# Chunked attention and a low-rank mixer on one core: W2's odd blocks moved, sums split by product, turns in place, attention's order placed anew

## The chip, the cores and the metric

The kernel runs on one core of a Trainium2 chip. The metric is the device time of one execution in microseconds (us); the median of 3 runs of the kernel before is 1055.16 us (1054.91 to 1055.36).

## What is computed

Attention within chunks of 64 positions, for 8 batches, 8 heads, 576 positions and a head size of 64; its output, 576 x 512 per batch, is x of a mixer. The mixer adds a product of rank 32 along the positions, then a two-layer ReLU network along the 512 channels with 2048 hidden ones:

```python
scores = scale * np.matmul(q_c, k_c.transpose(0, 1, 2, 4, 3))
scores = scores - np.max(scores, axis=-1, keepdims=True)
attn = np.exp(scores)
attn = attn / (np.sum(attn, axis=-1, keepdims=True) + 1e-09)
out = np.matmul(attn, v_c)
...
h = xt @ U @ V
u = x + h.transpose(0, 2, 1)
ch = np.maximum(u @ w_ch1, 0.0) @ w_ch2
return (u + ch).astype(np.float32)
```

q, k and v are float32; U, V and both weights come as float64 words and are turned to float32 in the kernel.

## The kernel before

**Tiles and groups.** Two batches make a pair (pr 0 to 3) of 1152 rows: nine tiles of 128 rows, three groups of three tiles. The hidden channels are 16 blocks f of 128. Every float32 product is made as three products in the matmul's float32r type: each operand is split into a high part (ScalarE, ACT, copies it) and the rest (VectorE, DVE, subtracts), and high x high, high x low and low x high are summed in a PSUM bank.

**Stages.** Pair 0's attention, the conversion of the weights and pair 0's first two groups come first, in an order that a planner inside the kernel makes (`order`, L144). From then on the program runs in ticks. `agenda` (L1042) is a dictionary from a tick to functions; `at` (L1046) enters one, and `tick` (L1180) runs those of the current tick after each step of TensorE (PE). So a tick is a place in the program's order, and with that a place in the queue of every engine; it is no time. Each engine, and each engine's queue of DMA issues, works in this order, and what waits holds all that is behind it. Ticks 128 to 256 run group (0, 2) and group (1, 0), 16 blocks each of `hidden` (L887, 12 matmuls) and `project_out` (L913, 9 matmuls), from weights that stay in SBUF.

**Joints.** The other eight groups are worked two at a time in four joints of 128 ticks each (`joint`, L1188; JOINT, L1074), from tick 256 to 768. There the first layer is a 2 x 2 block product with seven products in place of eight (1 to 7; the step A1 is product 1 of pair of blocks A). A joint has four chunks; a chunk has 14 such products of six matmuls (L1280) and 12 steps Ga, Gb of the second layer (L1257). Both operands of the seven products are sums of blocks. Those of W1 are made once: `combos` (L1080) has GpSimd (POOL) make the sums (L1098 to L1103), ACT and DVE split them (L1108, L1109), and SP (SyncE's queue) stores them to memory as `wc` (L1110); `plain_parts` (L1117) stores the blocks that need no sum. All eight use one pair of rooms, with 512 of each room's columns for the sums and 512 for their high parts. In the joints these operands are streamed back, 368 blocks in all through 11 windows (`window`, L1126; `issue`, L1134). Seven windows are two pieces of SBUF, the end of W1's area in an even and in an odd block, so a block takes two transfers (L1141); four are one piece (L1144).

The operands of u live in the first part of the same areas (`combo`, L1149). `u_combos` (L1153) makes them for one tile of the next joint: four sums on POOL (L1170 to L1173), then for each of the seven a copy (L1177) and a subtraction (L1178). Between two joints it is called three times, in the last chunk, after the steps Gb0, Ga2 and Ga3 (L1296).

**Attention of pairs 1 to 3** runs beside all this. `permute` (L681) rewrites q and k in memory by blocks of 32, issued from ACT. A tile (class Tile, L695) is loaded (L705), turned on DVE from qn to qT and kn to kT (L713), and at a visit (`visit`, L1312, at the ticks of VISITS, L1302) scored (L730); its softmax follows on DVE and ACT (L739). `turn_ex` (L759) turns ex into exb; `put_ex` (L765) stores it and `get_ex` (L772) reads it back as eT, both from SP; `load_v` (L715) is issued from POOL. At the next visit `values` (L779) takes eT, and `scaled` (L792) gives x. `spill` (L802) stores x; `fetch` (L841) reads it back for the mixer's sum `add` (L649), after which `turn` (L855), `put` (L862) and `get` (L869) bring u into shape, and `store` (L845) keeps it until `residual` (L1192) reads it as xr. The tiles of attention and of the mixer (qn, kn, qT, kT, ex, exb, vn, eT, xh, xl, xb, uf, us) come from one pool of nine slots, x from one of nine; a tile of a pool waits until the tile that last had its place is done with.

## Time and profile before

| what | value |
|---|---|
| median of 3 runs | 1055.16 us |
| the profiled execution's own time | 1051.83 us |
| its span | 1050.1 us |
| mean granted TensorE clock | 0.935 |
| PE, DVE, ACT, POOL busy, share of the span | 88%, 56%, 29%, 16% |
| DMA | 198.77 MB, mean 189 GB/s |

Times in the profile are microseconds from the start of the span. PE is TensorE's matmuls, PEld its weight loads, SPq (ACTq, POOLq) the DMA issues of that engine's queue. A granted clock of 1.00 is 2.4 GHz and 0.50 is 1.2 GHz; a value between them is a mean over a stretch. An engine's idle time is put down to what released it. The profiled execution is one execution; its durations are used for the sums, and its own time lies 3.33 us below the median.

### The profile page before, as it was taken

To read this page: it belongs to the slowest core of one execution; us is meant where nothing else is said; L and a number is where in the kernel's file an instruction comes from. 1 tells how busy PE (TensorE), PEld (TensorE's weight loads), DVE (VectorE), ACT (ScalarE), POOL (GpSimd) and SP (SyncE) were. 2 spreads that over 40 slices of the span, in tenths; PEclk is the share of its full clock that TensorE was granted. 3 is DMA by queue.
4 is the path that set the end of the run, shared out by engine and by line. 5 is a ranking of instruction groups with operands and counts; after the bars stand their busy time and mean duration, and the time that the engine had idled before them with its cause. 6 is when DMAs were issued, how large, how long until landed. Compare 5 with 4: busy or idle time off the path is not lost.

```text
span 1050.1 us, 17589 instructions
## 1 busy us (share of the span) xinstructions
PE 924.7 (88%) x6404; PEld 805.6 (77%) x6404; DVE 589.2 (56%) x1142; ACT 306.1 (29%) x600; POOL 167.6 (16%) x253
## 2 busy tenths in 40 slices
PE   6899999985869698978599778888978999999998
PEld 5689888764757587967498667777867988899987
DVE  5899965662546366645355474546664444753333
ACT  5666621221212013312022141222233221522211
POOL 4200001345441013201000140101050000300000
PEclk9999999987879889988799889988989999999999
DMA  9975857567779975969776896837669447674311
GB/s 185 219 248 157 223 107 152 150 190 173 184 232 285 267 216 157 288 166 246 173 209 168 224 275 168 225 95 206 183 208 278 153 132 210 210 240 139 111 62 61
DMA packets 362789, 198.77 MB, mean 189 GB/s; under 512 B 214384, under 2 KB 327568, under 8 KB 362704
## 3 DMA queue, kind: packets, MB, share of 16 engines
q1 hardware_dynamic: 247104, 174.78, 58.0%
q10 hardware_dynamic: 111360, 14.16, 8.8%
q0 software_dynamic: 4240, 8.71, 3.0%
q8 instruction: 51, 0.84, 0.3%
q14 instruction: 34, 0.28, 0.1%
HBM read 145.93 MB, written 65.80 MB: 202 GB/s over the span
## 4 chain that ended last, share of the span: by engine, by line
PE 43%; DMA 10%; SPq 4%; DVE 2%; issue 1%; POOL 1%; ACT 0%; DVEq 0%; ACTq 0%; POOLq 0%
PE o L1257 20%; DMA w<-wc 2%; SPq L775 2%; DMA eT<-exs 2%; DMA kblocks<-in_k_dram 2%; PE x_1A L1280 2%; PE x_0A L1280 1%; PE x_2A L1280 1%; PE x_1B L1280 1%; PE x_2B L1280 1%; PE x_3A L1280 1%; PE x_0B L1280 1%; DMA xb<-xd 1%; PE x_3B L1280 1%; DMA exs<-exb 1%
## 5 line engine op out<-in xcount | busy, mean ns | idle before, releaser
L895 PE MATMUL h<-uth,w 128*128 128x384 f32 x512 | 145.5, 350 | 14.3 <-DVE x L795 9.2
L720 POOL DMA_DIRECT2D vn<-in_v_dram x108 | 66.1, 620 | 427.2 <-PE as L730 120.1
L921 PE MATMUL o<-w,hh 128*128 128x512 f32 x384 | 126.0, 410 | 8.3 <-ACT hh L903 8.2
L1265 DVE TENSOR_TENSOR xr<-o,xr 128x512 f32<-128x512 f32 x96 | 65.0, 687 | 92.7 <-PE o L1257 92.4
L895 PEld LDWEIGHTS h<-uth,w 128*128 128x128 f32 x512 | 98.1, 196 | 18.6 <-issue 11.1
L921 PEld LDWEIGHTS o<-w,hh 128*128 128x128 f32 x384 | 74.1, 197 | 22.2 <-ACT hh L903 9.6
L895 PE MATMUL h<-utl,w 128*128 128x384 f32 x256 | 89.3, 349 | 0.9 <-DVE utl L885 0.9
L921 PE MATMUL o<-w,hl 128*128 128x512 f32 x192 | 78.8, 411 | 10.1 <-DVE hl L908 10.1
L903 ACT ACTIVATE hh<-h 128x384 fp32r<-128x384 f32 x64 | 31.1, 490 | 107.5 <-PE h L895 93.3
L750 ACT ACTIVATE ex<-ex 128x512 f32<-128x512 f32 x27 | 17.0, 631 | 145.6 <-DVE ex L744 128.9
L783 PE MATMUL as<-vn,eT 64*64 64x64 f32 x864 | 26.9, 264 | 36.2 <-DMA eT<-exs 31.4
L921 PEld LDWEIGHTS o<-w,hl 128*128 128x128 f32 x192 | 37.6, 196 | 22.0 <-DVE hl L908 13.4
L783 PEld LDWEIGHTS as<-vn,eT 64*64 64x64 f32 x864 | 23.0, 172 | 39.2 <-issue 33.4
L895 PEld LDWEIGHTS h<-utl,w 128*128 128x128 f32 x256 | 50.3, 197 | 3.5 <-DVE utl L885 1.2
L908 DVE SCALAR_TENSOR_TENSOR hl<-h,hh 128x384 fp32r<-128x384 f32 x64 | 34.7, 545 | 28.3 <-ACT hh L903 28.0
L1170 POOL TENSOR_TENSOR us<-uf 128x256 f32<-128x256 f32 x12 | 9.8, 813 | 248.5 <-DMA exs<-exb 121.0
L743 DVE TENSOR_REDUCE mx<-as 128x4 f32<-128x256 f32 x54 | 22.5, 417 | 45.4 <-PE as L783 43.8
L713 DVE STREAM_TRANSPOSE qT<-qn 128x512 f32<-128x512 f32 x27 | 19.0, 703 | 36.2 <-DMA qn<-qblocks 25.8
L1280 PE MATMUL x_0A<-w,w 128*128 128x384 f32 x92 | 22.0, 369 | 13.0 <-ACT w L1177 12.1
L1257 PE MATMUL o<-w,hh_1B 128*128 128x512 f32 x96 | 33.4, 432 | 0.0
L1178 DVE TENSOR_TENSOR w<-us,w 128x256 fp32r<-128x256 f32 x48 | 27.5, 601 | 10.5 <-ACT w L1177 10.5
L1257 PE MATMUL o<-w,hh_0B 128*128 128x512 f32 x96 | 33.0, 427 | 0.0
(326 smaller groups left out, 2080.8 us busy)
## 6 DMA issues: line engine op xcount, KB each, us to landing
w<-wc SPq DMA_DIRECT2D x288, 128.0 KB, 3.3
w<-wc SPq DMA_DIRECT2D x80, 256.0 KB, 3.9
wraw<-in_moe_w_ch_dram SPq DMA_DIRECT2D x32, 512.0 KB, 5.4
xs<-xb SPq DMA_DIRECT2D x120, 64.0 KB, 2.6
uf<-xs SPq DMA_DIRECT2D x30, 256.0 KB, 3.9
qblocks<-in_q_dram ACTq DMA_DIRECT2D x24, 288.0 KB, 5.5
kblocks<-in_k_dram ACTq DMA_DIRECT2D x24, 288.0 KB, 5.0
vn<-in_v_dram POOLq DMA_DIRECT2D x108, 64.0 KB, 4.1
```

What stands on the lines that cost most here:

```text
L720: nc.gpsimd.dma_start(self.vn[e * C : (e + 1) * C, c], v[b + 2 * self.pr, HP * e : HP * (e + 1), s0 : s0 + C, :].rearrange("h s d -> s h d"),)
L743: nc.vector.reduce_max(mx[:, e], self.sc[e].rearrange("p (h k) -> p h k", k=C), axis=AX.X)
L775: nc.sync.dma_start(self.eT[:, :, a, :], self.room[:, :, a].rearrange("g k (h i) -> (g k) h i", i=TB))
L783: nc.tensor.matmul(ps[e][cs, (HP + hp) * C : (HP + hp + 1) * C], lhsT=self.eT[rows, hp, 2 * c : 2 * c + 2, :].rearrange("p a i -> p (a i)" ...
L895: nc.tensor.matmul(ps[:, :GN], lhsT=w[:, z, cc], rhs=u[:, cc, :], start=(n == 0), stop=(n == 3 * NCC - 1))
L903: nc.scalar.activation(hh, ps[:, :GN], AF.Relu)
L908: nc.vector.scalar_tensor_tensor(hl, ps[:, :GN], 0.0, hh, op0=ALU.max, op1=ALU.subtract)
L921: nc.tensor.matmul(acc[j], lhsT=h[:, js], rhs=w2[f][:, z], start=(first and i == 0), stop=(final and i == 2),)
L1178: nc.vector.tensor_sub(to(k, 1), x, to(k, 0))
L1257: nc.tensor.matmul(acc[j], lhsT=u[:, q, js], rhs=w2[f][:, p], start=(z == "A" and e == 0 and n == 0), stop=(z == "B" and e == 1 and n == 2),)
L1265: nc.vector.tensor_add(xs[j], acc[j], xs[j])
L1280: nc.tensor.matmul(ps, lhsT=w[wz][:, cc], rhs=u[uz][:, cc], start=(k in (1, 2, 5) and cc == 0 and m == 0), stop=(cc == 1 and m == 2), skip ...
```

## The change

Seven things are edited. (1) `gather` copies W2's odd blocks, 512 KB each, into the W1 area of the even block before, once that area's last product is issued. The odd block is then free as a whole: u's operands take its first three quarters and a window of the stream its last quarter, so a window is one piece and `issue` makes one transfer of 256 KB. The first seven windows are filled one by one. (2) The sums of W1 use one half of the rooms and the other in turn; the 512 columns for the high parts stay common. (3) `u_combos` becomes `sum` and `split`, for one tile and one product each; between joints they stand after the last use of that product's operands in the last chunk. (4) `turn` and `turn_ex` write over their input. (5) The visits from (3, 0) on move from ticks 340, 404, 436, 468, 532 and 564 to 324, 343, 404, 436, 468 and 532, and ticks of permutations and mixes move with them. (6) A table, TUNE, shifts some 500 of the entries of `agenda` by fractions of a tick up to 25 ticks; entries of one tick are sorted by the fraction. On average fetches come 5.6 ticks sooner, spills 6.8 later, puts 2.8 later and residuals 9.1 later; the final visit goes to 548.75. (7) The table also names a queue for single transfers and an engine for single subtractions: fetches are issued from POOL but for (2, 0), on ACT, and (3, 7), on SP; some ten other transfers of the attention, three streamed blocks and some eight subtractions or sums go to POOL or ACT. Assertions on the order leave no instruction in the program.

```diff
+TUNE = {
+    "shift": {
+        "cget 0.0.0": 2, "cget 0.0.1": 1.25, "cget 0.0.2": -1, "cget 0.1.0": 3, "cget 0.1.1": -3,
...
+        "eturn 2_8": -2, "eturn 3_5": 0.5, "eturn 3_8": 1, "fetch 1.3": -7, "fetch 1.4": -16.75,
+        "fetch 1.5": -2, "fetch 1.6": -2.25, "fetch 1.8": 0.25, "fetch 2.0": 1, "fetch 2.1": -6.25,
+        "fetch 2.2": -13.25, "fetch 2.3": -7, "fetch 2.4": -3.5, "fetch 2.5": -5,
+        "fetch 2.6": -15.25, "fetch 2.7": 4, "fetch 2.8": -3, "fetch 3.0": -3, "fetch 3.1": -3,
...
+        "put 3.8": 4.5, "res 0.0": 7.5, "res 0.1": 7.5, "res 0.2": 6.5, "res 0.3": 7.5,
...
+        "spill 1_4": -0.25, "spill 1_5": 3.75, "spill 1_7": 7, "spill 1_8": 6, "spill 2_0": 4,
+        "spill 2_1": 13, "spill 2_2": 4.25, "spill 2_3": 5, "spill 2_4": 7, "spill 2_5": 4.5,
...
+        "clo 2.0.2": "S", "clo 2.0.3": "S", "clo 2.1.4": "P", "clo 2.2.1": "P", "clo 2.2.4": "S",
+        "clo 3.0.5": "S", "clo 3.1.3": "S", "clo 3.2.4": "P", "fetch": "P", "fetch 1_1": "S",
+        "fetch 1_2": "A", "fetch 1_4": "P", "fetch 1_7": "P", "fetch 2_0": "A", "fetch 2_2": "P",
+        "fetch 2_4": "P", "fetch 2_8": "P", "fetch 3_0": "P", "fetch 3_2": "P", "fetch 3_6": "P",
...
+    QUEUES = {"vn": "P", "perm": "A", **TUNE.get("queues", {})}
+
+    def dma(kind, dst, src, n=None):
+        way = QUEUES.get(f"{kind} {n}", QUEUES.get(kind, "S"))
+        {"S": nc.sync, "P": nc.gpsimd, "A": nc.scalar}[way].dma_start(dst, src)
+
+    def side(kind, n):
+        return nc.gpsimd if QUEUES.get(f"{kind} {n}", QUEUES.get(kind)) == "P" else nc.vector
...
         def turn(self):
-            self.qk = [slot(F32, z + "T_" + self.n, (P, HP, P)) for z in "qk"]
-            for dst, src in zip(self.qk, self.raw):
-                nc.vector.transpose(dst.rearrange("p a b -> p (a b)"), src.rearrange("p a i d -> p (a i d)"))
+            for z in self.raw:
+                z = z.rearrange("p a i d -> p (a i d)")
+                nc.vector.transpose(z, z)
+            self.qk = [z.rearrange("p a i d -> p a (i d)") for z in self.raw]
...
         def turn_ex(self):
-            self.exb = slot(F32, "exb_" + self.n, (P, NQ, HP * TB))
-            nc.vector.transpose(
-                self.exb.rearrange("p g x -> p (g x)"), self.ex.rearrange("p e b h k -> p (e b h k)")
-            )
+            assert self.sm is not None
+            ex = self.ex.rearrange("p e b h k -> p (e b h k)")
+            nc.vector.transpose(ex, ex)
+            self.exb = ex.rearrange("p (g x) -> p g x", g=NQ)
...
+    def at(key, s, *runs):
+        keys.add(key)
+        s += SHIFT.get(key, 0)
+        TUNE.get("ticks", {})[key] = s
         if s < FIRST and s % 4 < 2:
             s += 2 - s % 4
-        agenda.setdefault(s, []).extend(runs)
+        for run in runs:
+            agenda.setdefault(int(s // 1), []).append((s, run))
...
-            one, two = (b.bitcast(F32)[:, DM : 2 * DM] for b in st["b"])
+            one, two = (b.bitcast(F32)[:, i % 2 * 2 * DM :][:, 0:DM] for b in st["b"])
...
-                h, b = t[:, 0:DM], t[:, DM : 2 * DM]
+                h, b = t[:, DM : 2 * DM], t[:, i % 2 * 2 * DM :][:, 0:DM]
                 nc.scalar.copy(h, b.bitcast(F32))
-                nc.vector.tensor_sub(b, b.bitcast(F32), h)
+                side("wlo", i).tensor_sub(b, b.bitcast(F32), h)
                 nc.sync.dma_start(
                     wc[i][k : k + 2].rearrange("k p z x -> p z k x"),
-                    t[:, 0 : 2 * DM].bitcast(F32).rearrange("p (z k x) -> p z k x", z=2, k=2),
+                    t[:, i % 2 * DM :][:, 0 : 2 * DM].bitcast(F32).rearrange("p (z k x) -> p z k x", z=2, k=2),
...
+    def gather(i):
+        assert ("plain", i) in done and ("sum", i) in done and ("hidden", 1, 0, 2 * i) in done
+        done.add(("gather", i))
+        even, odd = (whole[f] for f in (2 * i, 2 * i + 1))
+        dma("gather", even[:, 0 : 2 * DM].bitcast(F32), odd[:, 2 * DM :].bitcast(F32))
+        moved[2 * i + 1] = even[:, 0 : 2 * DM].rearrange("p (s x) -> p s x", s=2)
+
+    moved = {}
+
     def window(n):
         k = n % LOADS
         if k < 7:
-            return [area[2 * k + z][:, 3 * KC :] for z in range(2)]
-        k -= 7
-        a = area[2 * 7 + k // 2][:, (k % 2) * 2 * KC : (k % 2 + 1) * 2 * KC]
-        return [a[:, 0:KC], a[:, KC:]]
+            return whole[2 * k + 1][:, 6 * KC : 8 * KC]
+        return whole[NF - 1][:, (k - 7) * 2 * KC : (k - 6) * 2 * KC]
...
-        src = wc[i][KEPT[k]]
-        if n % LOADS < 7:
-            for z, dst in enumerate(window(n)):
-                nc.sync.dma_start(dst.bitcast(F32), src[:, z])
-        else:
-            k = n % LOADS - 7
-            nc.sync.dma_start(
-                area[2 * 7 + k // 2][:, (k % 2) * 2 * KC : (k % 2 + 1) * 2 * KC].bitcast(F32),
-                src.rearrange("p z x -> p (z x)"),
-            )
+        done.add(("issue", n))
+        assert ("plain", i) in done and ("parts", i) in done
+        z = min(n % LOADS, 7)
+        assert ("gather", z) in done and (z == 7 or ("out", 1, 0, 2 * z + 1) in done)
+        assert n < LOADS or ("product", n - LOADS) in done
+        dma("w", window(n).bitcast(F32), wc[i][KEPT[k]].rearrange("p z x -> p (z x)"), n)
...
-        return [area[2 * i + z][:, 0 : 2 * GN].rearrange("p (c t) -> p c t", c=2) for z in range(2)]
-
-    def u_combos(j, a, b, ks=COMBOS):
-        def to(k, z):
-            return combo(k)[z][:, :, j * P : (j + 1) * P].rearrange("p c (a t) -> p a c t", t=TB)
+        return [whole[2 * i + 1][:, z * 2 * GN : (z + 1) * 2 * GN].rearrange("p (c t) -> p c t", c=2) for z in range(2)]
...
+        def sum(self, j, k):
+            assert all((self.s, j, z) not in self.sums for z in {3: (5,), 7: (6,)}.get(k, ()))
+            assert all(("sum", self.s, j, z) in done for z in {6: (5,), 3: (5, 6), 7: (6, 3)}.get(k, ()))
+            done.add(("sum", self.s, j, k))
+            self.sums[self.s, j, k] = self.plain(j, k)
+
+        def split(self, j, k):
+            i = COMBOS.index(k)
+            done.add(("split", self.s, j, k))
+            assert ("gather", i) in done and ("out", 1, 0, 2 * i + 1) in done
+            assert not self.s or ("last", self.s - 1, k) in done
+            x = self.sums.pop((self.s, j, k))
+            h, l = (
+                v[:, :, j * P : (j + 1) * P].rearrange("p c (a t) -> p a c t", t=TB) for v in combo(k)
+            )
+            nc.scalar.copy(h, x)
+            side("clo", f"{self.s}.{j}.{k}").tensor_sub(l, x, h)
...
-                                lhsT=w[wz][:, cc],
+                                lhsT=w[:, wz ^ low_first, cc],
...
-                if c == CHUNKS - 1 and s + 1 < len(JOINT) and step in ("Gb0", "Ga2", "Ga3"):
-                    j = ("Gb0", "Ga2", "Ga3").index(step)
-                    a, b = JOINT[s + 1]
-                    u_combos(j, mixes[a[0], GT * a[1] + j], mixes[b[0], GT * b[1] + j])
...
-        (340, 3, 0), (404, 3, 2), (436, 3, 4), (468, 3, 6), (532, 3, 8),
+        (324, 3, 0), (343, 3, 2), (404, 3, 4), (436, 3, 6), (468, 3, 8),
     ]
     chain = [(s, [Tile(pr, t) for t in range(t0, min(t0 + 2, NT))]) for s, pr, t0 in VISITS]
-    chain.append((564, []))
+    chain.append((532, []))
...
-                at(s1 + d, a.turn_ex)
-                at(s1 + 2 + d, a.sums)
-                at(s1 + 2 + d, a.put_ex)
-                at(max(s1 + 5, after - 14) + z, a.load_v)
-                at(max(s1 + 7, after - 12) + z, a.get_ex)
+                at("sums " + a.n, s1 + d, a.sums)
+                at("eturn " + a.n, s1 + 1 + d, a.turn_ex)
+                at("eput " + a.n, s1 + 2 + d, a.put_ex)
+                at("vn " + a.n, max(s1 + 5, after - 14) + z, a.load_v)
+                at("eget " + a.n, max(s1 + 7, after - 12) + z, a.get_ex)
...
-    for (pr, e), s in {(2, 0): 136, (2, 1): 180, (3, 0): 280, (3, 1): 340}.items():
+    for (pr, e), s in {(2, 0): 136, (2, 1): 180, (3, 0): 262, (3, 1): 330}.items():
...
-        (2, 4): 350, (2, 5): 353, (2, 6): 356, (2, 7): 359, (2, 8): 362,
-        (3, 0): 478, (3, 1): 481, (3, 2): 484, (3, 3): 487,
+        (2, 4): 333, (2, 5): 336, (2, 6): 390, (2, 7): 393, (2, 8): 396,
+        (3, 0): 447, (3, 1): 450, (3, 2): 453, (3, 3): 560,
...
+        at(f"wsum {i}", FIRST + 6 * i, sums)
+        at(f"wpart {i}", FIRST + 6 * i + 5, parts)
+        at(f"wplain {i}", 182 + 5 * i, lambda i=i: plain_parts(i))
+        at(f"gather {i}", 192 + 8 * i + 4, lambda i=i: gather(i))
...
+                t = base + BSTEP[k] + 1
+                at(f"csum {s}.{j}.{k}", t - 3 if k == 5 else t - 1, lambda m=m, j=j, k=k: m.sum(j, k))
+                at(f"csplit {s}.{j}.{k}", t, lambda m=m, j=j, k=k: m.split(j, k))
+    for n in range(7):
+        at(f"first {n}", 192 + 8 * n + 14, lambda n=n: issue(n))
```

## Rows read from the trace of the kernel before

**Rows 1.** The page, part 1: TensorE's busy time, share of the span and instructions.
```profile
PE 924.7 (88%) x6404; PEld 805.6 (77%) x6404; DVE 589.2 (56%) x1142; ACT 306.1 (29%) x600; POOL 167.6 (16%) x253
```

**Rows 2.** Six stretches: length, busy us (instructions) per engine, granted clock, DMA share, GB/s.
```profile
0.00:204.20 204.20, 189.27 (x1622) 159.49 (x1623) 156.03 (x292) 101.20 (x156) 27.82 (x65) 1.00 0.73 179
204.20:424.50 220.30, 173.19 (x1396) 149.74 (x1395) 115.89 (x241) 46.10 (x95) 75.95 (x97) 0.87 0.82 214
424.50:611.50 187.00, 152.04 (x976) 132.64 (x974) 95.92 (x195) 42.60 (x92) 18.95 (x29) 0.89 0.80 213
611.50:780.00 168.50, 148.47 (x1026) 130.19 (x1026) 95.58 (x194) 44.67 (x99) 24.82 (x37) 0.92 0.70 193
780.00:920.70 140.70, 136.24 (x765) 121.04 (x766) 76.48 (x140) 41.84 (x97) 20.01 (x28) 0.97 0.64 191
920.70:1050.10 129.40, 125.44 (x625) 112.47 (x623) 49.31 (x85) 29.70 (x64) 0.00 (x0) 1.00 0.39 122
```

**Rows 3.** The chain that ended last, joint 3's second chunk: start, us, what.
```profile
952.08 1.07 PE x_1A L1280 x6
...
983.43 1.07 PE x_2A L1280 x6
```

**Rows 4.** What PE waited for, 204.2 to 1050: us in total, times, longest.
```profile
PE as L783 <- DMA eT<-exs: 31.4, 18, 8.8
PE x_0A L1280 <- ACT w L1177: 12.1, 2, 7.1
PE o L921 <- DVE hl L908: 9.8, 2, 9.5
PE h L895 <- DVE x L795: 9.2, 4, 6.5
PE o L921 <- ACT hh L903: 7.6, 1, 7.6
...
PE x_3B L1280 <- ACT u_3B L1212: 5.8, 2, 5.4
PE h L895 <- DVE x L649: 5.1, 1, 5.1
PE as L783 <- DVE hl L908: 4.8, 1, 4.8
PE x_1B L1280 <- ACT u_1B L1212: 4.8, 1, 4.8
```

**Rows 5.** POOL's sums of W1 (L1098), who waited for L1103, and ACT's timeline.
```profile
L1098 POOL TENSOR_TENSOR wch<-w x8: 1272/1280/1313, 204.3 to 295.4; 128x512 f32<-128x512 f32 x8
...
  DMA wc<-wch: 31.5, 6
...
  ACT wch L1108: 46.6, 7
...
250.09 0.62 ACT L1108 CAST wch<-wch 128x512 fp32r<-128x512 f32 x1 [12.75 <-DMA eT<-exs]
```

**Rows 6.** DVE's timeline before PE's longest wait for hl: [idle before, releaser].
```profile
365.01 0.71 DVE L713 STREAM_TRANSPOSE qT<-qn 128x512 f32<-128x512 f32 x1 [9.58 <-DMA xs<-xb]
```

**Rows 7.** PE's timeline at the start of joint 1.
```profile
611.51 0.69 PE L1280 MATMUL x_0A<-w,w 128*128 128x384 f32 x1 [7.09 <-ACT w L1177]
```

**Rows 8.** The page, part 6: streamed blocks in two pieces, KB each, us to landing.
```profile
w<-wc SPq DMA_DIRECT2D x288, 128.0 KB, 3.3
```

**Rows 9.** SP's issues before PE's wait for eT at 685.21: start, us, count.
```profile
677.63 1.82 SPq L1141 DMA_DIRECT2D w<-wc  x4
679.54 5.33 SPq L775 DMA_DIRECT2D eT<-exs  x8
```

**Rows 10.** DVE's timeline: the mixer's sum of a fetched tile.
```profile
490.42 0.69 DVE L649 TENSOR_TENSOR xb<-u,xb 128x512 f32<-128x512 f32 x1 [3.78 <-DMA xb<-xd]
```

**Rows 11.** The page, part 5: POOL's issues of v's reads: busy, mean ns | idle before.
```profile
L720 POOL DMA_DIRECT2D vn<-in_v_dram x108 | 66.1, 620 | 427.2 <-PE as L730 120.1
```

**Rows 12.** The page, part 4: the chain that ended last, shares by engine.
```profile
PE 43%; DMA 10%; SPq 4%; DVE 2%; issue 1%; POOL 1%; ACT 0%; DVEq 0%; ACTq 0%; POOLq 0%
```

More of the change, by code (lines that the diff above doesn't have):

```diff
@@ L767, in put_ex @@
             for a in range(NQ):
[L768 to L769 removed]
+                dma(
+                    "putex",
+                    self.room[:, :, a].rearrange("g k x -> k g x"), self.exb[a * TB : (a + 1) * TB], self.n
                 )
@@ L852, in add @@
         def add(self):
+            assert (self.pr, self.t) not in kept_x or ("fetch", self.n) in done
+            done.add(("mix", self.n))
             self.ops[1].run()
         def turn(self):
+            assert ("mix", self.n) in done
             self.xb = slot(F32, "xb_" + self.n, (P, NQ, NCC * TB))
@@ L864, in put @@
             for a in range(NQ):
-                nc.sync.dma_start(
-                    self.room[:, :, a].rearrange("g k x -> k g x"), self.xb[a * TB : (a + 1) * TB]
+                dma(
+                    "put",
+                    self.room[:, :, a].rearrange("g k x -> k g x"), self.xb[a * TB : (a + 1) * TB], self.n
                 )
@@ L887, in hidden @@
     def hidden(pr, g, f):
+        done.add(("hidden", pr, g, f))
         uh, ul = ut_of[pr, g]
@@ L914, in project_out @@
         hh, hl = hs
+        if j == GT - 1:
+            done.add(("out", pr, g, f))
         t = g * GT + j
@@ L1117, in plain_parts @@
     def plain_parts(i):
+        assert ("gather", i) not in done
+        done.add(("plain", i))
         one, two = (area[f].bitcast(F32).rearrange("p (z k x) -> p z k x", z=2, k=2) for f in (2 * i, 2 * i + 1))
@@ L1180, in tick @@
     def tick():
         nonlocal now
-        for run in agenda.pop(now, ()):
+        for _, run in sorted(agenda.pop(now, ()), key=lambda z: z[0]):
             run()
@@ L1273, in joint @@
                     loads[0] += 1
-                    w = [v.rearrange("p (c f) -> p c f", c=2) for v in window(n)]
+                    w = window(n).rearrange("p (z c f) -> p z c f", z=2, c=2)
+                    low_first = KEPT[k] > 2 and not (2 * c + "AB".index(z)) % 2
                     u = combo(k)
@@ L1287, in joint @@
                             )
+                    assert ("issue", n) in done and all(("split", s, i, k) in done for i in range(GT))
+                    done.add(("product", n))
+                    if c == CHUNKS - 1 and z == "B":
+                        done.add(("last", s, k))
                     issue(n + LOADS)
@@ L1330 @@
         start = s - 15 if len(now) == 1 else s - 19 if ahead < 24 or ahead > 30 else s - ahead + 1
+        n = f" {now[0].n if now else 0}"
+        s += SHIFT.get("visit" + n, 0)
+        keys.add("visit" + n)
+        TUNE.get("ticks", {})["visit" + n] = s
         for z, a in enumerate(now):
-            at(start if z == 0 else s - 13, a.load)
-            at(max(start + 6, s - 13) if z == 0 else s - 7 if i else s - 4, a.turn)
-        at(s, lambda prev=prev, now=now: visit(prev, now))
+            at("load " + a.n, start if z == 0 else s - 13, a.load)
+            at("turn " + a.n, max(start + 6, s - 13) if z == 0 else s - 7 if i else s - 4, a.turn)
@@ L1403 @@
             pend = (pr, g, f, hs)
+    w2.update({f: moved[f] for f in range(1, NF, 2)})
     for n in range(7, LOADS):
```

161 lines of the change are left out of this document (97 added, 64 removed), and 124 rows, old and new, of the table TUNE.

## The prediction

> **What bounds the kernel now.** I read the stretches first, then TensorE's waits, then what stood ahead of the engine that was waited for. Of the 1050.1 us span PE is busy 924.7 us [rows 1]. The six stretches say where the rest is [rows 2]. The lead (to 204.2) and the last joint (from 920.7) run at full clock, granted 1.00. Between them, from 204.2 to 920.7, the granted clock is 0.87, 0.89, 0.92 and 0.97, and PE lacks 47.1, 35.0, 20.0 and 4.5 us of being busy: 106.6 us. A mixed figure below 1.00 is time at 1.2 GHz beside time at 2.4 GHz, and in each of these stretches PE had idled.
>
> How good can a joint be? A clean chunk lasts from 952.08 to 983.43, 31.35 us [rows 3], four of them 125.4. The joints took 187.0, 168.5, 140.7 and, with the tail, 129.4. So joints 0 and 1 are 61.6 and 43.1 above the clean ones, partly attention's own products; joint 2 only 15.3. There is little to win at the end and much from 204 to 780.
>
> Idle time costs more than itself. In joints 0 and 1 PE idles 55.0 us; the clock means 2 x 0.11 x 187.0 + 2 x 0.08 x 168.5 = 68 us at 1.2 GHz [rows 2]. If all the idle lies inside the slow time, 13 us of work ran at half speed and lost 6.5; if none does, 68 us of work lost 34. I take the middle, 20 us lost for 55 idle, and multiply idle time by 1.4 below; ends 1.1 and 1.6.
>
> **The change, part by part.** The waits behind the 106.6 us are few and long [rows 4].
>
> Weight sums, 204 to 308. POOL makes the eight sums of W1's blocks in one pair of rooms, so each waits until the last pair has gone to memory (31.5 us in 6 waits). They start from 204.3 to 295.4, 13.0 us apart. ACT's cast of a sum is queued ahead of its relu, waits 46.6 us for POOL in all, once 12.75 [rows 5]; then PE waits for hh (7.6), and through DVE's subtraction behind the same cast for x (6.5), x again (5.1) and hl (4.8): 24.0 us. The change alternates two rooms for the sums, but both keep one room for the high part, so ACT's next cast still waits for the store. I take two thirds: 16 x 1.4 = 22; ends 0 and 24 x 1.6 = 38.
>
> Turns in place. A tile of attention takes three tiles fewer (qT, kT, exb) from the pool of nine slots. At 365.01 DVE stood 9.58 us because its turn needed a slot that a put had not left [rows 6]; that is PE's 9.5 us for hl. The transposes themselves keep their count and shapes: nothing. I take 10 of 9.5 x 1.4 = 13; ends 0 and 15.
>
> u's sums product by product. Before, three bursts stand between two joints, and PE waits 12.1 us for x_0A's operands, 7.09 of it at 611.51 [rows 4, 7]. Now each product's copy follows the last use of its room, under the last chunk. The same copies and subtractions then sit between relus of that chunk, where ACT and DVE are busy 42.6 of 187.0 and 95.9 of 187.0 us in joint 0 [rows 2]; this cover is wide. 12.1 x 1.4 = 17; I take 15; ends 0 and 19.
>
> Streamed blocks in one transfer. 288 issues of 128 KB become 144 of 256 KB [rows 8]. An issue takes SP 1.82 / 4 = 0.455 us [rows 9], so SP is spared 144 x 0.455 = 66 us between 424 and 1046. On its queue stand attention's reads: PE waits 31.4 us in 18 waits for eT [rows 4]. Before one of them SP issues exs, four blocks and then eight reads of eT for 5.33 us without a pause [rows 9]. Half the blocks, puts and spills placed later, and slots that come free sooner should halve these waits: 31.4 / 2 x 1.4 = 22, and 3 more because moved spills and residuals no longer stand ahead: 25. Ends: -10 (reads placed too late) and 31.4 x 1.6 = 50. The eight copies of W2's odd blocks (512 KB each) are new on SP: eight issues of about 0.6 us, and each holds SP until PE's last use of the even W1 and the store before it. No row shows such a wait; ends 0 and, like the longest of eT's, 8.8 us each for those that meet a read. They fall where pair 1 still runs from resident weights, so I take nothing.
>
> Fetches. DVE's add stood 3.78 us for a fetched tile at 490.42 [rows 10], and c_1B and u_1B behind it; PE waits 5.8 and 4.8 us for such u [rows 4]. Fetches go to POOL and on average some five ticks earlier. 10.6 x 1.4 = 15; I take 9; ends -5 and 17.
>
> What is added. Four visits instead of three fall in joint 0, and joint 2 keeps one: moved work, but joint 0 is the fullest in DMA (share 0.80 [rows 2]). POOL takes 22 of the 24 fetches at 0.62 us, 14 us in all [rows 11], and a few subtractions; a fetch waiting for one of nine x tiles holds the sums behind it, for which ACT's and DVE's split waits, and then PE. I charge 8 us, about one long wait with its slow clock; ends 0 and 40.
>
> **Sum:** 22 + 10 + 15 + 25 + 9 - 8 = 73 us. The profiled execution took 1051.83 us, 1.73 around its span, and the runs' median is 1055.16, 3.33 more; I take the difference from the median: 1055.16 - 73 = 982. A measurement of this kernel can tell about 0.2%, 2 us, from no change.
>
> **The rivals.** *All named stalls go:* 38 + 15 + 19 + 50 + 17 would be 139, less what the attention products in between still need; with the middle factor, 34 + 13 + 17 + 44 + 15 = 123, so about 930, between 920 and 955. For it: each wait has a part of the change that points at it. Against it: a tick is only a place in each queue, and a wait removed shows the next.
>
> *The transfers themselves are late, not their issue.* The DMA engines' mean share is 0.82 and 0.80 in the two worst stretches [rows 2]; if eT is late because packets queue there, only the weight sums, the turns and the transitions gain, and about half of what I gave them: 24, or up to 40 where joint 2 follows; 1015 to 1040, say 1030. For it: joint 0 gets a fourth visit's transfers, and the bytes are not fewer. Against it: four blocks and eight reads issue back to back for 7.2 us before a wait of PE [rows 9]. The chain that ended last gives DMA 10% and SP's issue 4% of the span [rows 12], so the issue itself is some 42 us of the path; 2 in 10. The Trainium skill, DMA: Bandwidth & Descriptors, section Issuing engines are not separate DMA queues, speaks for this rival: it says that DMAs issued from several engines run on the same 16 DMA engines, so that spreading them saves only the sequencer's issue time, usually small beside the transfer. By that rule the 25 and 9 us would be near nothing. The chain's 4% is not small here, so the trace bears the rule out in part only.
>
> *Slower: POOL becomes the queue that holds the joints.* In joints 0 to 2 POOL now carries v's reads, the fetches and all sums of u in one order. Its waits are harmless today (427.2 us idle before v's reads [rows 11]) since little behind it is urgent. If a fetch waits for an x tile and sums stand behind it, the split of that product is late, ACT waits, the relus behind wait, and PE. At 8.8 us a wait x 1.4 = 12 us each; it eats the 81 us of gains from the seventh blocked fetch on, and at nine of the 22 gives 1055 - 81 + 9 x 12 = 1082; with the part gains of the second rival two or three suffice, 1060. Against it: residuals are placed later, which leaves x tiles to the fetches. 8 in 100.
>
> *It does not do what it says:* gains and new waits cancel, 1053 to 1057; 3 in 100.
>
> **How the numbers follow.** The forecast (955 to 1010) has 0.54, all stalls gone 0.15, transfers late 0.20, no change 0.03, slower 0.08. Faster by over 0.2%: 0.54 + 0.15 + 0.20 = 0.89; within 0.03; slower 0.08. The range reaches into both neighbours: 935 leaves out about 0.06 of the best case, 1038 leaves out the slower cases and a little of the third, 0.13: together 0.19.
>
> **What would show it.** Right: the stretch of the weight sums shortens by some 20 us and ACT's wait for POOL's sums falls well below 46.6; no 9 us wait of a turn for a slot; x_0A of joints 1 and 2 follows the last o product without an idle row; no row of 128 KB w transfers is left; PE's wait for eT falls to about 16; granted clock 0.93 or more from 204 to 780. Wrong: eT's wait stays near 31 with SP idle before it (transfers late); new rows with POOL's sums or splits as releaser of ACT and PE (POOL holds); or a long wait of SP at the copies of W2's odd blocks.

## The result and the profile after

Three runs of the changed kernel take 1019.12 us in the median (1010.12 to 1021.43), beside 1055.16 before: ratio 0.9637, 95% interval 0.9547 to 0.9728. The gain is 36 us; 73 were forecast, and 1019 lies in the range (935 to 1038). The profiled execution has a span of 1019.6 us and a granted clock of 0.956 (0.935 before).

Below is the page of the changed kernel: its busy line, which answers to [rows 1], the shares of the chain that ended last [rows 12], the streamed blocks [rows 8], and the fetches that POOL now issues.

```profile
PE 917.1 (90%) x6404; PEld 796.1 (78%) x6404; DVE 592.5 (58%) x1134; ACT 300.8 (29%) x600; POOL 213.0 (21%) x318
...
PE 49%; DMA 10%; DVE 5%; SPq 4%; issue 1%; ACT 1%; ACTq 0%; DVEq 0%
...
L217 POOL DMA_DIRECT2D xb<-xd x22 | 12.2, 556 | 135.3 <-DMA xd<-x 30.8
...
w<-wc SPq DMA_DIRECT2D x220, 256.0 KB, 3.7
```

No 128 KB transfer of w is left. The stream is 224 blocks, not 368: before, they took 368 transfers (288 of 128 KB and 80 of 256 KB), now 224, of which four go out from ACT and POOL. The shares of DMA and of SP's issues in the chain are what they were; DVE's rose from 2% to 5%. Next, the stretches of the changed kernel with the columns of [rows 2]; they end where joints 0, 1, 2 and 3 begin, and with the span.

```profile
204.20:416.90 212.70, 171.74 (x1394) 147.38 (x1394) 121.23 (x234) 45.31 (x92) 93.40 (x119) 0.90 0.90 242
416.90:596.60 179.70, 152.91 (x1105) 132.20 (x1104) 110.48 (x230) 45.83 (x105) 41.93 (x64) 0.92 0.90 239
596.60:757.70 161.10, 146.16 (x997) 127.53 (x997) 92.45 (x184) 42.47 (x97) 27.62 (x41) 0.95 0.70 198
757.70:890.10 132.40, 130.30 (x667) 116.06 (x666) 65.74 (x116) 36.77 (x87) 16.56 (x24) 0.99 0.59 187
890.10:1019.60 129.50, 125.52 (x625) 112.54 (x623) 47.16 (x80) 29.57 (x64) 1.01 (x1) 0.99 0.37 118
```

Against [rows 2] the stretch before the joints is shorter by 7.6 us, joint 0 by 7.3, joint 1 by 7.4, joint 2 by 8.3. PE lacks 41.0, 26.8, 14.9 and 2.1 us of being busy in them, 84.8 in place of 106.6. These 21.8 us less idle came with 30.6 us less time, a factor of 1.4, as the prediction took (1.3 in a second profile: 20.5 and 27.5 us); what was wrong is how much idle time would go. In the two worst stretches the DMA engines' share is now 0.90, from 0.82 and 0.80, and the granted clock there is 0.90 and 0.92, where 0.93 or more was named.

What PE waited for in the changed kernel, 204.2 to the end (total, times, longest), beside [rows 4]:

```profile
PE as L949 <- DMA eT<-exs: 21.9, 20, 3.5
PE y L991 <- ACT xh L974: 9.3, 1, 9.3
...
PE x_3B L1495 <- ACT u_3B L1426: 8.4, 3, 3.8
PE h L1070 <- DVE x L961: 7.9, 3, 5.6
PE as L949 <- DVE hl L1083: 7.3, 1, 7.3
...
PE x_2B L1495 <- ACT u_2B L1426: 2.4, 1, 2.4
```

The 12.1 us for the operands of x_0A are gone, and eT's wait has shrunk. In their place stand 9.3 us for xh, the copy that is the high part of x, and a longer wait for the copies u_3B and u_2B, which ACT makes of a product before PE may go on. (x, u, c and y with a number and a letter belong to a joint's chunk 0 to 3 and pair of blocks A or B: x_0A is a joint's first product. hh and hl are the high and low part of a relu's result.)

### The profile page after: what moved, and what is told of

Read it like the earlier page. It is cut to its first block, busy times and chain, and to the rows that moved or that the text cites. A ratio compares the mean times of both kernels' runs of the same rounds, so it can differ in the third digit from the quotient of the medians.

```text
span 1019.6 us, 17395 instructions
## 1 busy us (share of the span) xinstructions
PE 917.1 (90%) x6404; PEld 796.1 (78%) x6404; DVE 592.5 (58%) x1134; ACT 300.8 (29%) x600; POOL 213.0 (21%) x318
## 4 chain that ended last, share of the span: by engine, by line
PE 49%; DMA 10%; DVE 5%; SPq 4%; issue 1%; ACT 1%; ACTq 0%; DVEq 0%
PE o L1471 23%; SPq L217 4%; PE o L1098 3%; DMA eT<-exs 3%; DMA w<-wc 3%; PE h L1070 3%; PE x_0B L1495 2%; PE x_1A L1495 2%; PE x_0A L1495 1%; PE x_2A L1495 1%; PE x_1B L1495 1%; DVE w L1392 1%; PE x_3A L1495 1%; PE x_3B L1495 1%; PE as L949 1%
## 5 line engine op out<-in xcount | busy, mean ns | idle before, releaser
L1098 PE MATMUL o<-w,hh 128*128 128x512 f32 x384 | 124.2, 405 | 2.2 <-ACT hh L1078 2.2
L217 POOL DMA_DIRECT2D vn<-in_v_dram x104 | 63.9, 625 | 221.0 <-PE as L894 136.8
L1070 PEld LDWEIGHTS h<-uth,w 128*128 128x128 f32 x512 | 98.0, 196 | 11.5 <-issue 9.3
L1098 PEld LDWEIGHTS o<-w,hh 128*128 128x128 f32 x384 | 72.6, 193 | 15.7 <-ACT hh L1078 3.5
L1098 PE MATMUL o<-w,hl 128*128 128x512 f32 x192 | 78.2, 407 | 1.9 <-DVE hl L1083 1.9
L949 PE MATMUL as<-vn,eT 64*64 64x64 f32 x864 | 26.4, 252 | 32.2 <-DMA eT<-exs 21.9
L1098 PEld LDWEIGHTS o<-w,hl 128*128 128x128 f32 x192 | 36.9, 192 | 13.9 <-DVE hl L1083 5.5
L217 POOL DMA_DIRECT2D xb<-xd x22 | 12.2, 556 | 135.3 <-DMA xd<-x 30.8
L874 DVE STREAM_TRANSPOSE qn<-qn 128x512 f32<-128x512 f32 x27 | 19.0, 704 | 31.1 <-DMA qn<-qblocks 28.8
L1471 PE MATMUL o<-w,hh_3B 128*128 128x512 f32 x96 | 32.5, 422 | 0.0
L1471 PE MATMUL o<-w,hh_0A 128*128 128x512 f32 x96 | 31.8, 414 | 0.0
L1471 PE MATMUL o<-w,hh_1A 128*128 128x512 f32 x96 | 31.5, 410 | 0.0
```

The source lines that it names most:

```text
L217: {"S": nc.sync, "P": nc.gpsimd, "A": nc.scalar}[way].dma_start(dst, src)
L874: nc.vector.transpose(z, z)
L949: nc.tensor.matmul(ps[e][cs, (HP + hp) * C : (HP + hp + 1) * C], lhsT=self.eT[rows, hp, 2 * c : 2 * c + 2, :].rearrange("p a i -> p (a i)" ...
L1070: nc.tensor.matmul(ps[:, :GN], lhsT=w[:, z, cc], rhs=u[:, cc, :], start=(n == 0), stop=(n == 3 * NCC - 1))
L1098: nc.tensor.matmul(acc[j], lhsT=h[:, js], rhs=w2[f][:, z], start=(first and i == 0), stop=(final and i == 2),)
L1471: nc.tensor.matmul(acc[j], lhsT=u[:, q, js], rhs=w2[f][:, p], start=(z == "A" and e == 0 and n == 0), stop=(z == "B" and e == 1 and n == 2),)
```

## The experiments

Every kernel ran beside the kernel before on the same chip, but the kernels are spread over several chips; so ratios are compared here and not times. One execution of a kernel tells only so much about a stretch: a second profile of the changed kernel itself gives 209.1, 182.8, 165.0 and 132.1 us from 204.2 to joint 3, against 212.7, 179.7, 161.1 and 132.4 above. Differences under 4 us in one stretch aren't read, unless several kernels repeat them.

**The changed kernel again**, for a closer ratio.

> The changed kernel itself once more, beside the others on one chip: a ratio to the kernel before of 0.96 to 0.97, about 1019 us. The spread between its own runs (1010 to 1021) says what a comparison here can tell.

Measured: 1022.33 us (6 runs, 1016.05 to 1027.31), ratio 0.9677 (0.964 to 0.9714). The runs of this kernel spread over 1.1%. Those of the kernel before, beside it, spread over 0.9% (1050.68 to 1060.26), so the 0.2% that the prediction took from three runs was too fine.

**Two rooms alone**, put into the kernel before:

```diff
-            one, two = (b.bitcast(F32)[:, DM : 2 * DM] for b in st["b"])
+            one, two = (b.bitcast(F32)[:, i % 2 * 2 * DM :][:, 0:DM] for b in st["b"])
...
-                h, b = t[:, 0:DM], t[:, DM : 2 * DM]
+                h, b = t[:, DM : 2 * DM], t[:, i % 2 * 2 * DM :][:, 0:DM]
```

> The kernel before with the two rooms alone. Theory (the second room is worth its 20 us by itself): ACT's waits for POOL's sums fall from 46.6 us to under 20, 1032 to 1042 us. Rival (it needs its place in the order too: ACT's next cast then waits for the store of the common room instead): 1048 us or more.

Measured: 1036.72 us, ratio 0.9813 (0.9785 to 0.9842): 20 us. Its stretch before the joints, and who waited for its casts and sums of W1 and for what, to be read against [rows 2, 5]:

```profile
204.20:406.40 202.20, 165.46 (x1389) 142.94 (x1388) 121.73 (x239) 46.61 (x95) 78.31 (x96) 0.92 0.89 232
```

```profile
  DMA wc<-wch: 21.0, 5
...
  DMA wc<-wcl: 5.2, 5
...
  POOL wch L1103: 2.1, 1
```

The stretch fell from 220.3 to 202.2 us, and joint 0 hardly (187.0 to 184.8). ACT's 46.6 us for POOL's sums are down to 2.1; in its place ACT waits for the stores of the high parts, which keep one room.

**One room in the changed kernel**, the same step from the other end. Its sums 1, 3, 5 and 6 are made over the sum before, ahead of the split of that one, so those parts of the weights are not the reference's.

```diff
-            one, two = (b.bitcast(F32)[:, i % 2 * 2 * DM :][:, 0:DM] for b in st["b"])
+            one, two = (b.bitcast(F32)[:, 0:DM] for b in st["b"])
...
-                h, b = t[:, DM : 2 * DM], t[:, i % 2 * 2 * DM :][:, 0:DM]
+                h, b = t[:, DM : 2 * DM], t[:, 0:DM]
```

> The changed kernel with one pair of rooms for W1's sums again. Theory (the second room took the waits of ACT for POOL out of the stretch from 204 to 308 us): POOL's sums wait for each store again, ACT's casts wait 30 us or more for POOL, and the time is 1034 to 1044 us. Rival (the common room of the high parts holds the chain nearly as much, so that little was won there): 1019 to 1025 us.

Measured: 1042.16 us, ratio 0.9847 (0.9809 to 0.9884), 18 to 22 us behind the changed kernel by the ratios. Its stretch before the joints and, among those who waited for POOL's sums, ACT's cast:

```profile
204.20:434.70 230.50, 171.38 (x1396) 148.33 (x1395) 113.76 (x234) 45.10 (x91) 90.32 (x118) 0.87 0.84 223
```

```profile
  ACT wch L1296: 49.0, 5
```

From both ends the rooms are worth about 20 us, nearly all in this stretch, and the wait is the one named in [rows 5].

**Turns in place**, added to the kernel before with two rooms:

```diff
-            self.qk = [slot(F32, z + "T_" + self.n, (P, HP, P)) for z in "qk"]
...
+            for z in self.raw:
+                z = z.rearrange("p a i d -> p (a i d)")
+                nc.vector.transpose(z, z)
```

> The kernel before with two rooms and, added to that, the turns of attention in place (its sums then stand ahead of the turn of ex in the same tick). Theory (a tile fewer per turn only passes the missing slot on to the next taker): DVE's 9 us wait of a turn is gone, another wait for a slot stands near it, and the time is within 5 us of the two rooms alone, ratio 0.977 to 0.986. Rival (the freed slots were worth the 10 us that the prediction gave them): ratio 0.968 to 0.975.

Measured: 1026.42 us, ratio 0.9729 (0.969 to 0.9768); 9 us less than with the rooms alone, and the intervals are apart. DVE's longest wait of a turn for a slot, 10.6 us with the rooms alone, is gone, and PE's wait of the second layer's products o for hl falls from 11.4 to 4.4 us. But the stretch in which both stood is hardly shorter, 201.9 us (its row is shown with the next kernel) beside 202.2, so this is not where the 9 us came from. Where they came from no run shows: the two profiles differ by 4.0 us in all. The turn of q and k was not undone by itself within the changed kernel.

**Streamed blocks whole**, added to that: W2's odd blocks are copied, the first seven windows are filled early, and each block is one transfer. This is the changed kernel with an empty table, u's sums in three bursts as before (that edit is shown below), and the visits, mixes, permutes and reads of u at their old ticks. Two things come along that were not tried singly: the sums of u of a tile share one slot of the pool where they had two, so that sums 3 and 7 wait for the splits of 5 and 6, and the turn of ex stands one tick later.

```diff
+    TUNE.clear()
     QUEUES = {"vn": "P", "perm": "A", **TUNE.get("queues", {})}
...
-        (324, 3, 0), (343, 3, 2), (404, 3, 4), (436, 3, 6), (468, 3, 8),
+        (340, 3, 0), (404, 3, 2), (436, 3, 4), (468, 3, 6), (532, 3, 8),
...
-                at(f"cget {s}.{z}.{j}", base - 1 + j + z if s else end - 18 + 4 * j, lambda m=m, j=j, z=z: m.get(j, z))
+                at(f"cget {s}.{z}.{j}", end - 23 + 4 * j if s else end - 18 + 4 * j, lambda m=m, j=j, z=z: m.get(j, z))
```

> That kernel with, added to it, W2's odd blocks moved and one transfer per streamed block: the changed kernel with an empty table, u's sums in three bursts, and visits, permutations, mixes and reads of u at the ticks of before. Theory (144 issues fewer are worth 11 to 15 us in the joints, the eight copies cost some of it before the joints): ratio 0.965 to 0.976 with the last stretch before the joints 5 us longer. Rival (the copies and what waits for them cost what the issues save): 0.977 to 0.986.

Measured: 1021.9 us, ratio 0.9675 (0.9641 to 0.9708), 6 us less by the ratios, with intervals that overlap. The stretches of the kernel with rooms and turns in place, then of this one (204.2 to joint 3):

```profile
204.20:406.10 201.90, 168.45 (x1397) 145.07 (x1398) 125.82 (x244) 46.61 (x95) 77.03 (x96) 0.92 0.89 233
406.10:589.60 183.50, 153.60 (x977) 133.49 (x975) 96.35 (x195) 42.65 (x92) 18.89 (x29) 0.90 0.82 217
589.60:756.50 166.90, 149.78 (x1026) 130.16 (x1026) 95.59 (x194) 44.94 (x99) 24.71 (x37) 0.93 0.68 195
756.50:896.30 139.80, 134.85 (x765) 119.11 (x766) 76.26 (x140) 42.04 (x96) 19.75 (x28) 0.99 0.64 192
```

```profile
204.20:417.60 213.40, 172.24 (x1397) 148.44 (x1397) 128.36 (x245) 46.70 (x95) 77.02 (x96) 0.90 0.89 240
417.60:593.80 176.20, 149.47 (x977) 130.55 (x975) 96.66 (x194) 42.36 (x92) 19.06 (x30) 0.92 0.83 227
593.80:749.80 156.00, 144.79 (x1027) 126.48 (x1027) 96.55 (x196) 44.78 (x99) 23.79 (x37) 0.96 0.71 208
749.80:890.50 140.70, 136.55 (x765) 121.17 (x766) 75.99 (x138) 40.67 (x93) 17.57 (x26) 0.96 0.63 189
```

Joints 0 and 1 win 7.3 and 10.9 us, and the stretch ahead of them loses 11.5. The timelines of SP, DVE and PE of the second kernel show one place of that loss:

```profile
345.56 6.32 SPq L218 DMA_DIRECT2D eT<-exs  x4
...
352.47 0.43 SPq L218 DMA_DIRECT2D xb<-xd  x1
```

```profile
355.91 0.69 DVE L803 TENSOR_TENSOR xb<-u,xb 128x512 f32<-128x512 f32 x1 [7.41 <-DMA xb<-xd]
```

```profile
356.66 1.01 PE L895 MATMUL as<-kn,qn 64*64 64x64 f32 x26 [8.59 <-DVE xb L803]
```

Four reads of eT hold SP for 6.32 us; the fetch of a mixer's tile stands behind them, DVE waits 7.41 us for it, and PE's next products of attention wait 8.59 us for DVE. The copies and the first fills are new on SP's queue ahead of that place. That they made SP late there was not tried by itself, and the rows above allow another cause: the stretch moves 47.0 MB in the first kernel (201.9 us at 233 GB/s) and 51.2 MB in the second (213.4 at 240), 4.2 MB more, as much as the eight copies of 512 KB, at the same DMA share of 0.89. So the DMA engines themselves may have made it longer; no run separates the two.

**Two transfers again** in the changed kernel, for the windows that were split before:

```diff
-        dma("w", window(n).bitcast(F32), wc[i][KEPT[k]].rearrange("p z x -> p (z x)"), n)
+        src = wc[i][KEPT[k]]
+        if n % LOADS < 7:
+            for z in range(2):
+                dma("w", window(n)[:, z * KC : (z + 1) * KC].bitcast(F32), src[:, z], n)
...
```

> The changed kernel, but each streamed block for the first seven windows in two transfers of 128 KB on the same queue; everything else, W2's copies too, as it is. Theory (SP's issue time was what made eT late): 144 issues of 0.39 us are back, 56 us of SP's time, and PE's wait for eT rises from 21.9 us towards 31: 1029 to 1040 us. Rival (the transfers themselves are late, not their issue): within 4 us of 1019, eT's wait unchanged.

Measured: 1032.76 us, ratio 0.9785 (0.9757 to 0.9814), 11 to 16 us behind the changed kernel (0.9677 and 0.9637). Its page shows the split, and its waits of PE the surprise:

```profile
w<-wc SPq DMA_DIRECT2D x282, 128.0 KB, 3.2
```

```profile
PE as L949 <- DMA eT<-exs: 22.3, 21, 3.7
```

The time came back, the wait for eT did not: 22.3 us here, 21.9 and 25.0 in the two profiles of the changed kernel. Its profiled execution was the shortest of its runs, 1026.65 us, so the profile shows little of the loss (joint 1 took 170.2 us, against 161.1 and 165.0). Through which waits the second transfer costs its 11 to 16 us stays open. Nor is it only the issue that changed. The bytes are the same, but they go in more and smaller packets (this run, then the changed kernel):

```profile
DMA packets 350406, 202.97 MB, mean 198 GB/s; under 512 B 204784, under 2 KB 315152, under 8 KB 350320
```

```profile
DMA packets 329796, 202.94 MB, mean 199 GB/s; under 512 B 202480, under 2 KB 276240, under 8 KB 329712
```

**The moved visits**, with mixes, permutes and reads of u, added to the kernel with streamed blocks whole; this is the changed kernel with an empty table and u's sums in bursts. Its diff is `TUNE.clear()` and the bursts' edit, shown below.

> That kernel with, added to it, the visits, permutations, mixes and reads of u at the ticks of the changed kernel, table still empty, u's sums still in bursts. Theory (an earlier attention empties joint 2 and crowds joint 0; the sum is small): joint 2 shorter by 5 to 8 us, joint 0 longer by as much, ratio within 0.005 of the kernel without the move. Rival (clean borders come from the earlier mixes): both waits of x_0A at the borders are gone here and present without the move, 10 to 15 us faster. Beside the kernel with the empty table and sums by product (ratio 0.980): the bursts are 4 to 8 us faster there too.

Measured: 1022.69 us, ratio 0.9689 (0.9652 to 0.9725), no difference from the kernel without it. Three of its stretches, joints 0 to 2:

```profile
415.40:597.90 182.50, 155.58 (x1105) 134.49 (x1104) 106.86 (x222) 44.42 (x99) 25.05 (x38) 0.92 0.84 225
597.90:763.30 165.40, 143.73 (x997) 125.86 (x996) 94.83 (x188) 43.51 (x97) 24.09 (x37) 0.94 0.67 199
763.30:891.90 128.60, 128.60 (x667) 115.04 (x665) 68.04 (x118) 37.72 (x87) 11.82 (x17) 1.00 0.62 195
```

Joint 2 fell by 12.1 us, and PE is busy in all of it; joints 0 and 1 rose by 6.3 and 9.4. PE's wait for the operands of x_0A (11.0 us without the moves) is gone although the sums still come in bursts; 16.0 us for u_0B are new. The timelines of ACT and DVE name what held that copy the two times:

```profile
436.73 0.55 ACTq L218 DMA_DIRECT2D qblocks<-in_q_dram  x1
437.33 0.49 ACT L1438 ACTIVATE hh_0B<-c_0B 128x384 fp32r<-128x384 f32 x1 [5.49 <-DMA exs<-ex]
```

```profile
628.03 0.71 DVE L1030 STREAM_TRANSPOSE xb<-xb 128x512 f32<-128x512 f32 x1 [9.39 <-DMA xs<-xb]
```

At 436.73 a rewrite of q stands on ACT's queue ahead of a relu and holds ACT for 5.49 us; PE waits 4.08. At 628.03 a turn of the mixer holds DVE for 9.39 us, c_0B, hh_0B and u_0B stand behind it, and PE waits 11.89.

**The table emptied** in the changed kernel, u's sums product by product (`TUNE.clear()` is the whole edit):

> The changed kernel with an empty table: every entry of the agenda at its unshifted tick, every transfer on SP but for v's reads (POOL) and the permutations (ACT), every subtraction on DVE; two rooms, turns in place, sums by product, single transfers and the moved visits stay. Theory (the structural parts carry the gain, the table a little of it): 1019 plus 5 to 15, 1024 to 1034 us. Rival (the table carries it, since a part without a fitting order only moves the wait): 1045 us or more, with PE's waits for eT back at 25 us or more. Rival (the shifts are noise): within 5 us of 1019.

Measured: 1035.39 us, ratio 0.9796 (0.9744 to 0.9848). From the kernel just above it differs only in that u's sums follow product by product, and it is 11 us slower by the ratios; the intervals are apart. The table is worth 13 to 17 us to the changed kernel.

**Bursts in the changed kernel**, table kept:

```diff
-                t = base + BSTEP[k] + 1
-                at(f"csum {s}.{j}.{k}", t - 3 if k == 5 else t - 1, lambda m=m, j=j, k=k: m.sum(j, k))
-                at(f"csplit {s}.{j}.{k}", t, lambda m=m, j=j, k=k: m.split(j, k))
+                t = base + STEPS.index(("Gb0", "Ga2", "Ga3")[j]) + (1, 2, 3)[j]
+                for z, kk in enumerate((5, 6, 1, 2, -1, -5, -2, -6, 3, 7, -3, -7, 4, -4)):
+                    if abs(kk) == k:
+                        run = (lambda m=m, j=j, k=k: m.sum(j, k)) if kk > 0 else (lambda m=m, j=j, k=k: m.split(j, k))
+                        agenda.setdefault(t, []).append((t + z / 16, run))
```

> The changed kernel, but the sums and splits of u for joints 1 to 3 in three bursts after Gb0, Ga2 and Ga3 of the last chunk, as before, one burst per tile. Theory (the spread hides what stood between the joints): x_0A of joints 1 to 3 waits again for ACT's copies, 5 to 8 us each at two joints or three, with the slow clock 15 to 25 us in all: 1034 to 1044 us. Rival (the spread costs the last chunk what it saves at the border): within 4 us of 1019.

Measured: 1016.9 us, ratio 0.9612 (0.9576 to 0.9647), against 0.9637 and 0.9677: 3 to 7 us ahead of the changed kernel, with intervals that overlap. Against the kernel with bursts and an empty table (0.9689) the table is worth 8 us here, and the intervals are apart. One part of what product by product costs is seen in the changed kernel's timelines of PE and ACT near the end of joint 2:

```profile
873.34 1.34 PE L1495 MATMUL x_3B<-w,w 128*128 128x384 f32 x6 [2.10 <-ACT u_3B L1426]
```

```profile
870.24 1.02 ACT L1391 CAST w<-us 128x256 fp32r<-128x256 f32 x3
871.51 0.49 ACT L1437 ACTIVATE hh_3B<-c_3B 128x384 fp32r<-128x384 f32 x1 [0.25 <-DVE c_3B L1429]
871.90 1.00 ACT L1391 CAST w<-us 128x256 fp32r<-128x256 f32 x3
872.81 0.48 ACT L1426 COPY u_3B<-x_3B 128x384 f32<-128x384 f32 x1
```

Six copies of the next joint's operands stand on ACT right before the copy u_3B, and PE waits for that one. The same occurs at 580.00 (3.78 us) and 742.62 (2.56). With bursts no such row of x_3B is left, and joint 2 takes 129.1 us, in place of 132.4 and 132.1; the three kernels with bursts below have 129.0 each.

**Bursts, and the reads of u for joints 1 to 3 at the ticks of before** (`end - 23 + 4 * j`, their shifts dropped):

> The kernel of the bursts with the reads of u for joints 1 to 3 also at the ticks of before, ten to eighteen ticks later than in the changed kernel. Theory (the borders became clean because u is read early, not because its sums are spread): ACT's copies wait for these reads again, x_0A waits 5 to 7 us at two of three borders, and the time rises by 12 to 20 us over the bursts with early reads, to 1029 to 1037 us. Rival (order of reads does not matter, the puts of the mixer come early enough since the mixes moved): within 5 us of 1017.

Measured: 1012.33 us, ratio 0.9608 (0.9571 to 0.9646); beside it the changed kernel took 1022.33 (0.964 to 0.9714). No difference from the bursts alone, and no wait for x_0A's operands either: reading u earlier is not what took that wait away.

**Bursts, and two of the weight sums placed anew**, aimed at PE's waits of 7.4 us for hl and 5.8 for x in the stretch before the joints, as the kernel of the bursts has them:

```diff
+    TUNE["shift"].update({"wpart 5": 0, "wpart 6": -1})
```

> The kernel of the bursts with the fifth split of W1's sums three ticks later and the sixth three ticks earlier, so that no two follow each other closely. Theory (the common room of the high parts still holds ACT for a store, and through ACT and DVE cost PE 5.8 and 7.4 us there): both waits fall under 2 us and the time by 10 to 18 us, to 999 to 1007 us. Rival (a wait removed there shows the next one, or the DMA engines cannot run the stretch faster): 1012 us or more.

Measured: 1016.15 us, ratio 0.962 (0.9582 to 0.9657). Nothing gained: the waits moved (6.5 us of the rank-32 product for x, 26.3 in all for eT).

**Bursts, and no shift for what lies in ticks 128 to 256**, the part of the table before the joints:

> The kernel of the bursts with the whole table, but no shift for an entry whose tick lies from 128 to 256. Theory (the table's gain is in the joints, and before them the plain order is as good or better, as with the two rooms alone, where that stretch took 202 us against 209 to 213): the stretch to joint 0 is 203 to 207 us, the joints as in the kernel of the bursts, 1003 to 1010 us. Rival (the shifts there fit the copies and reads that are new): 1017 us or more.

Measured: 1016.39 us, ratio 0.9637 (0.9602 to 0.9671), not to be told from the bursts with the whole table; its stretch to joint 0 took 210.1 us, not 203 to 207. So no gain is shown for the table's shifts before the joints. That all of its gain lies in the joints is not shown either: the interval also overlaps that of the bursts with an empty table (0.9652 to 0.9725).

## Why the prediction was right or wrong

The range held, but the forecast did not: 1019 lies outside its own band of 955 to 1010, in that of the second rival (1015 to 1040), and about half of the 73 us came. Rooms and turns, forecast at 32, gave 29 of them; the other parts, forecast at 41 together, gave 5 to 10, as the sum of gains and losses of up to 17 us.

The kernels make a chain from before to after. PE's waits are summed over the rows of its view from 410 us on: for eT; for a copy u of a product (all rows "x_… <- ACT u_…"; in the changed kernel 8.4 + 2.4 + 1.4 + 1.4 + 0.4 = 14.0); and for ACT's and DVE's splits of x_0A's operands. From 204.2 us on, where the prediction's 31.4 is counted, the waits for eT are 31.4, 28.2, 23.0, 15.3, 21.5, 24.6, then 21.9 and 25.0, then 20.8.

| kernel | ratio | step, us | eT | u | x_0A |
|---|---|---|---|---|---|
| before | 1 | | 31.4 | 10.6 | 13.0 |
| two rooms | 0.9813 | -20 | 28.2 | 9.7 | 12.5 |
| + turns in place | 0.9729 | -9 | 23.0 | 11.7 | 11.5 |
| + streamed blocks whole | 0.9675 | -6 | 14.9 | 10.4 | 13.5 |
| + visits, mixes, reads moved | 0.9689 | +1 | 18.8 | 25.2 | none |
| + sums product by product | 0.9796 | +11 | 22.0 | 31.7 | none |
| + table = after | 0.9637, again 0.9677 | -17, -13 | 16.8, 19.4 | 14.0, 13.5 | none |
| after with bursts | 0.9612 | | 17.9 | 7.2 | none |

*Weight sums: right*, 22 forecast and 20 measured, from both ends. That the common room for the high parts keeps part of the wait was right too; in the changed kernel the casts and who waited for them read:

```profile
L1296 ACT CAST wch<-wch x8: 604/615/622, 212.1 to 290.6; 128x512 fp32r<-128x512 f32 x8
...
  DMA wc<-wch: 15.9, 2
...
  DMA wc<-wcl: 4.0, 3
```

*Turns in place: the size was right*, 10 and 9, the place was not: the wait named went, and its stretch stayed as long as it was (202.2 and 201.9 us), so the agreement of the two numbers is in part luck. In the changed kernel a stall like that of [rows 6] stands on ACT, which waits for the same kind of transfer, and PE's wait is as long as before:

```profile
366.89 1.14 ACT L974 CAST xh<-x 128x512 fp32r<-128x512 f32 x2 [9.51 <-DMA xs<-xb]
```

```profile
368.08 0.79 PE L991 MATMUL y<-xh,ust 128*128 128x512 f32 x1 [9.27 <-ACT xh L974]
```

*u's sums product by product: the step that failed.* "12.1 x 1.4 = 17; I take 15; ends 0 and 19" was wrong in sign. x_0A's wait went, but with the moved visits, mixes and reads while the sums still came in bursts; placing the sums product by product then cost 11 us, and with the table 3 to 7, where the intervals overlap. The mistake was "this cover is wide": it was read from ACT's and DVE's busy share, and what counts is the place in ACT's queue ahead of a copy that PE waits for. A lower end of 0 had shut a loss out. The waits for such copies account for 6.5 of the 11 us (25.2 to 31.7), some 9 with the factor 1.4; the rest was not traced.

*Streamed blocks: 25 forecast, 6 measured.* PE's wait for eT was to fall from 31.4 to about 16, and fell to 21.9 and 25.0 (16.8 and 19.4 without the stretch ahead of the joints). Rooms and turns alone had left 23.0, before SP's transfers were touched; that part was counted twice. The streamed blocks took it on to 15.3, half of what was forecast for them, and the moved visits raised it to 21.5 again (single profiles of each; the changed kernel's two differ by 3.1). And "They fall where pair 1 still runs from resident weights, so I take nothing", of the copies, failed: the step that has them loses 11.5 us ahead of the joints and wins 18.2 in joints 0 and 1. That sentence counted the issue of the copies and how long they hold SP, not their 4.2 MB on DMA engines that were busy to 0.89. Undoing the single transfer alone costs 11 to 16, without a longer wait for eT; so what a single transfer saves is not seen in the wait from which the 25 was worked out.

*Fetches: 9 forecast.* The wait at which they were aimed did go, DVE's for a fetched tile (total, times, longest; before, then the changed kernel, where the second profile has 6.5):

```profile
DVE xb L649 <- DMA xb<-xd: 19.1, 6, 5.2
```

```profile
DVE xb L802 <- DMA xb<-xd: 1.5, 1, 1.5
```

It was the table that took it, for with the table emptied it is still 18.3 us. But PE's waits for u, at 10.6 before, went up to 14.0: other work stands ahead of these copies. The step of the moved visits raised them to 25.2, the table took off about 18, and the sums product by product keep 7 of what is left; with bursts the two named, for u_3B and u_1B, are down from 5.8 and 4.8 to none and 1.9. Which entries of the table do it, the fetches on POOL or others, wasn't tried one by one.

*What is added: 8.* Some such waits came, but in the queues of ACT (a rewrite of q) and DVE (a turn of the mixer), and the table removed them. The step of the moved visits cost 1 us, which is within the noise.

*The rivals.* POOL as the queue that holds the joints did not come: PE's waits for POOL are 1.1 us in the changed kernel, and ACT's waits for POOL's sums of u are 7.2, from 24.3 before. "The transfers themselves are late" is not ruled out. The time lies in its band, rooms and turns alone give 29 of the 36 us, eT's wait ends at 21.9 and 25.0, about where these two left it, and the DMA share of 0.90 in two stretches is as that rival has it. Against it stand the step of the streamed blocks, where eT's wait fell from 23.0 to 15.3, and the run with two transfers, where the same bytes on the same queues cost 11 to 16 us more. But both change the packets with the issues, so neither shows that SP's issue time is what counts. The Trainium skill, DMA: Bandwidth & Descriptors, section Issuing engines are not separate DMA queues, holds the issue time to be usually small beside the transfer. The rows agree, with 0.455 us for an issue [rows 9] and 3.3 from issue to landing [rows 8]; what 144 issues fewer are worth by themselves, and what moving issues to another engine is worth, no run here shows.

## What to carry to other kernels

Ahead of work that "fits under" an engine, read which instruction of that engine the critical one waits for, and count what the new work puts in front of it: ACT was busy for 42.6 of 187.0 us in joint 0 [rows 2], and its order still gave back 11 us. Where several parts of a change point at one wait, count the wait once: rooms and turns had taken a quarter of eT's wait before the part meant for it. Count the bytes of a copy, and not only its issue, where the DMA engines are already busy. And test the parts of an order singly: the changed kernel with bursts (0.9608 to 0.9637 in four kernels) is at or slightly ahead of the change itself (0.9637, 0.9677).
